# The head of a Mamba2-and-MLP kernel: C of the first chunk in one transfer and turned by TensorE, weight loads issued by ScalarE, mixing moved up

## The chip, the cores and the metric

The kernel runs on one core of a Trainium2 chip. The metric is the device time of one execution in microseconds (us). Engine names in the profile: PE is TensorE's matmuls, PEld its weight loads, DVE is VectorE, ACT ScalarE, POOL GpSimd, SP SyncE, which issues most DMAs. "L585" is line 585 of the kernel before, and matmuls of fp32 leave two records each, as do their weight loads.

## The reference

Two blocks follow one another. A state-space block works on 4 batches, 8 heads, 768 positions, head size 32, state size 16; then an MLP works on 3,072 tokens of 256 values.

```python
# per chunk of the sequence; cum = cumsum of log(a) in the chunk
L  = exp(cum[i] - cum[j]) for i >= j, else 0
y  = ((C @ B.T) * L) @ x  +  (C @ state) * exp(cum)
state = exp(sum(log a)) * state + sum_j exp(cum[-1] - cum[j]) * B[j] x[j]
# MLP
h = y.reshape(3072, 256) @ w_in          # 256 x 2048
g = h * clip(h + 3, 0, 6) / 6
out = g @ w_out                          # 2048 x 256
```

x, B, C and the result are float32; w_in and w_out arrive as 64-bit floats.

## The kernel before

The work goes through six chunks of 128 positions, each with all 4 batches and 8 heads. A chunk is two halves of 64. Its state-space part gives 512 columns of y, and the MLP part of that chunk follows: 16 blocks of 128 hidden values (`mlp_in` for chunk 0, `lead` and `follow` later), then the products with w_out. TensorE goes through the MLP of chunk k while the other engines prepare chunk k+1.

The order on each engine is written out by hand (`manual_schedule`): every engine takes its instructions in the order in which the program issues them. What the change touches is the head, ahead of chunk 0's MLP (L969 to L1018), where nothing can hide behind earlier matmuls:

- `load_bc(c)` loads B and C. B of chunk 0 goes over ScalarE's DMA queue. C of chunk 0 comes "pairs first", with eight DMAs of 32 KB on SP (L104); VectorE then turns it with one 32x32 block transpose (`turn_squares`, L481) into csT, from which `part_heads` makes the two halves of cT (L488). Chunks 1 and 2 load C "tokens first" in one DMA (L97) and let TensorE transpose it (`turn_c`, L449).
- `diff_mask`, `diff` and `diff_exp` make the decays L of chunks 0 and 1 on TensorE and ScalarE: a mask, one matmul that subtracts, and 16 small ones per batch that add (L352, L364, L373), then exp (L381). `first_eto` does the same for the decay from the chunk's middle. Chunk 1's batches 2, 3 are exponentiated in the head, 0 and 1 during chunk 0's MLP.
- `add_up` is a scan on VectorE, first for chunks 0 and 1, later for the rest; `store_rows` writes the rest to DRAM, and `turn_cum` and `by_token` (L329, L332) turn it for later chunks.
- `ends` scales B by the decay on GpSimd (L412), `fade` scales csT by eto (L494), `scores` makes C B^T and the states (L543, L555), `multiply` puts the decays on (L585), `mix` makes y (L611 with x, L516 with the state), `keep` copies y to yT (L625), `renew` makes the new state.
- `load_w(i)` loads a megabyte of weights into one of three buffers: i = 0 to 3 the quarters of w_in, 4 to 7 those of w_out. `decode(i)` turns the 64-bit floats into fp32 in steps that `weights(i, n)` issues n at a time: a copy of the top 16 bits on ScalarE (L206), two masks on VectorE (L223, L225) and two instructions for the factor (L209, L213), two activations on ScalarE (L229, L231), then L236 and L249 on VectorE. Loads 4 and up are issued when the buffer's earlier user is decoded (L234).
- `busy` is a filler matmul of 128x512 into a free bank.
- PSUM tiles with the tags f0 to f3 share four banks; a new tile of a tag waits until the old one is read.

## Time and profile before

| | us |
|---|---|
| median of 3 runs | 345.6 (345.52 to 349.03) |
| the profiled execution | 345.45 |
| its span, first to last instruction | 343.7 |
| PE busy / share | 334.6 / 97% |
| VectorE busy / share | 220.1 / 64% |
| ScalarE busy / share | 173.2 / 50% |
| GpSimd busy / share | 142.7 / 42% |
| first L636 (chunk 0's MLP) starts | 22.98 |
| first L735 (chunk 0 times w_out) starts | 50.55 |

How to read it: times inside the profile count from the span's start. The chain of waits is followed back from the last instruction; its lines give start, length and what ran. A timeline line gives start, length, engine, line, operation, tiles, and in brackets how long the engine sat idle before it and what ended that. Busy shares are means over stages with different limits.

### The profile page before, as it was taken

What the parts mean: (1) busy time and instruction counts of PE and PEld (TensorE: products, weight loads), DVE (VectorE), ACT (ScalarE), POOL (GpSimd) and SP (SyncE); (2) the same over time, 40 slices, a digit from 0 to 9 for tenths busy, and PEclk for the clock granted to TensorE, in tenths of its full rate; (3) what the DMA queues carried; (4) which work ended last, traced back from release to release, by engine and by line L of the source; (5) the groups of instructions that cost most, each with busy time, mean ns of one, the idle gap of its engine ahead of it and who ended that gap; (6) DMA issues with size and microseconds to landing.
All of it is one profiled execution on the core that took longest, in us unless ns stands there. A gap on an engine that the chain in (4) does not pass through costs nothing.

```text
span 343.7 us, 8181 instructions
## 1 busy us (share of the span) xinstructions
PE 334.6 (97%) x3378; PEld 266.5 (78%) x3378; DVE 220.1 (64%) x357; ACT 173.2 (50%) x359; POOL 142.7 (42%) x139
## 2 busy tenths in 40 slices
PE   6889999999999999999999999999999999999996
PEld 2554448888778888888888888888887788888995
DVE  6689999999698647775438666447666324676011
ACT  4769878738874561564551564561564010565000
POOL 3300000093299923099611199610099400089500
PEclk9999999999999999999999999999999999999999
DMA  8888959206941057242029242051200010200010
GB/s 173 163 341 169 242 187 176 53 2 95 192 61 23 5 69 159 34 60 51 2 34 176 46 56 58 6 64 17 34 13 0 2 19 1 34 12 2 0 33 31
DMA packets 91605, 24.89 MB, mean 72 GB/s; under 512 B 84208, under 2 KB 87952, under 8 KB 91056
## 3 DMA queue, kind: packets, MB, share of 16 engines
q1 hardware_dynamic: 87184, 23.06, 34.8%
q10 hardware_dynamic: 4384, 1.31, 1.7%
q8 instruction: 26, 0.43, 0.5%
q14 instruction: 11, 0.09, 0.1%
HBM read 21.07 MB, written 3.29 MB: 71 GB/s over the span
## 4 chain that ended last, share of the span: by engine, by line
PE 75%; issue 11%; DMA 4%; DVE 2%; ACT 2%; POOL 2%; SPq 2%; POOLq 0%; DVEq 0%
PE h L684 31%; PE wb L861 13%; PE wc L861 8%; PE wa L861 8%; PE oa L794 4%; PE ob L794 4%; PE y L611 2%; PE y L516 2%; DMA raw<-in_moe_w_in_dram 2%; PE cb L543 2%; DMA eto<-cum_e 1%; ACT L L401 1%; POOL bs L412 1%; DMA pairs<-in_C_dram 1%; SPq L321 1%
## 5 line engine op out<-in xcount | busy, mean ns | idle before, releaser
L708 DVE SCALAR_TENSOR_TENSOR gT<-gT,h 128x512 f32<-128x512 f32 x80 | 54.9, 687 | 30.7 <-ACT gT L707 27.9
L707 ACT ACTIVATE gT<-h,half_up 128x512 f32<-128x512 f32 x80 | 55.1, 690 | 33.2 <-PE h L684 33.1
L780 POOL TENSOR_TENSOR s<-gT 128x512 f32<-128x512 f32 x20 | 25.8, 1288 | 66.4 <-DVE gT L708 66.4
L684 PE MATMUL h<-gap,w_gap 128*128 128x512 f32 x160 | 51.8, 409 | 0.0
L684 PE MATMUL h<-high,w_high 128*128 128x512 f32 x160 | 50.7, 398 | 0.1
L684 PE MATMUL h<-low,w_low 128*128 128x512 f32 x160 | 50.3, 395 | 0.0
L700 ACT ACTIVATE h<-h 128x512 f32<-128x512 f32 x40 | 23.5, 588 | 30.4 <-PE h L684 30.4
L684 PEld LDWEIGHTS h<-high,w_high 128*128 128x128 f32 x160 | 29.5, 188 | 8.5 <-DVE h L697 2.1
L684 PEld LDWEIGHTS h<-low,w_low 128*128 128x128 f32 x160 | 30.1, 188 | 7.2
L684 PEld LDWEIGHTS h<-gap,w_gap 128*128 128x128 f32 x160 | 29.9, 188 | 7.1 <-DVE gap L678 0.5
L401 ACT ACTIVATE L<-L,cum_n 128x64 f32<-128x64 f32 x128 | 31.6, 337 | 0.7 <-POOL L L162 0.7
L861 PE MATMUL wb<-s,w_out 128*128 128x256 f32 x128 | 30.7, 382 | 0.0
L419 POOL TENSOR_TENSOR tmp<-state,eto 128x256 f32<-128x256 f32 x5 | 3.6, 721 | 61.0 <-ACT eto L405 60.9
L735 PE MATMUL o<-w_out,gT 128*128 128x256 f32 x128 | 28.7, 381 | 0.0
L697 DVE TENSOR_SCALAR h<-h 128x512 f32<-128x512 f32 x40 | 27.7, 692 | 1.2 <-PE h L684 1.2
L636 PE MATMUL h<-yT,w 128*128 128x512 f32 x64 | 27.7, 594 | 0.0
L780 POOL TENSOR_TENSOR s<-s,gT 128x512 f32<-128x512 f32 x20 | 26.9, 1345 | 1.6
L585 DVE TENSOR_TENSOR L<-L,cb 128x512 f32<-128x512 f32 x24 | 15.3, 682 | 19.1 <-PE cb L543 16.3
L735 PEld LDWEIGHTS o<-w_out,gT 128*128 128x128 f32 x128 | 24.1, 190 | 3.8 <-issue 0.5
L861 PEld LDWEIGHTS wb<-s,w_out 128*128 128x128 f32 x128 | 24.0, 190 | 3.6
L412 POOL TENSOR_TENSOR bs<-B,L 128x128 f32<-128x128 f32 x24 | 13.7, 584 | 30.9 <-ACT L L401 25.8
L780 POOL TENSOR_TENSOR gT<-gT 128x512 f32<-128x512 f32 x20 | 25.9, 1294 | 0.0
(141 smaller groups left out, 534.3 us busy)
## 6 DMA issues: line engine op xcount, KB each, us to landing
raw<-in_moe_w_out_dram SPq DMA_DIRECT2D x4, 1024.0 KB
L<-cum_d SPq DMA_DIRECT2D x8, 512.0 KB
xt<-in_x_dram SPq DMA_DIRECT2D x6, 512.0 KB
raw<-in_moe_w_in_dram SPq DMA_DIRECT2D x3, 1024.0 KB
out_dram<-back SPq DMA_DIRECT2D x128, 16.0 KB
eto<-cum_e SPq DMA_DIRECT2D x20, 64.0 KB
B<-in_B_dram SPq DMA_DIRECT2D x5, 256.0 KB
raw<-in_moe_w_in_dram ACTq DMA_DIRECT2D x1, 1024.0 KB
```

The source lines that it names most:

```text
L401: nc.scalar.activation(Ls[c][:, b, h], Ls[c][:, b, h], AF.Exp, bias=cum_n[:, c, g:g + 1])
L412: nc.gpsimd.tensor_tensor(out=bss[c][:, hs], in0=Bs[c][:, hs], in1=Ls[c][:, b, :, HT - 1:HT].to_broadcast([P, NH, N]), op=ALU.mult)
L636: nc.tensor.matmul(out=h.rearrange("p r i -> p (r i)"), lhsT=first_in[f // FP][:, j, f % FP * P:(f % FP + 1) * P], rhs=yTs[k][:, j], start ...
L684: nc.tensor.matmul(out=h, lhsT=w[:, j, f * P:(f + 1) * P], rhs=y[:, j], start=(start and j == 0), stop=True, skip_group_check=True)
L697: nc.vector.tensor_scalar(out=h, in0=h, scalar1=-Z / UP, scalar2=None, op0=ALU.mult)
L700: nc.scalar.mul(h, h, -Z / UP)
L707: nc.scalar.activation(g, h, AF.Relu, bias=half_up, scale=UP * UP / 6.0)
L708: nc.vector.scalar_tensor_tensor(out=g, in0=g, scalar=UP, in1=h, op0=ALU.min, op1=ALU.mult)
L735: nc.tensor.matmul(out=o[:, b % 2], lhsT=gTs[0][:, f, b * P:(b + 1) * P], rhs=w_out[:, f], start=(f == 0 and b % 2 == 0), stop=True, skip_ ...
L780: nc.gpsimd.tensor_tensor(out=o, in0=p_, in1=q_, op=op)
L794: nc.tensor.matmul(out=bank[:, slot], lhsT=lhs[:, j], rhs=rhs[:, j], start=(clear and j == 0), stop=True, skip_group_check=True)
L861: nc.tensor.matmul(out=bank[:, slot], lhsT=lhs[:, j], rhs=rhs[:, j], start=(clear and j == 0), stop=True, skip_group_check=True)
```

## The change

C of chunk 0 is loaded tokens first in one DMA, as chunks 1 and 2 have it, and TensorE turns it, together with B and the later chunks' sums, behind the first half (batches 2, 3) of chunk 1's differences. The second half of those differences (batches 0, 1) moves from before the scores to before the mixing. GpSimd makes the second half of csT out of cT's two halves. The loads 1, 2, 3 are issued by ScalarE, not SP, and at other places. The factor's two instructions of decode 1 are issued with its first step, and this whole first step goes behind `keep`. `by_token` goes from VectorE to ScalarE. Mixing and copying alternate by halves. The fillers go.

```diff
-        if 0 < c < TURN:
+        if c < TURN:
             bcs[c] = [tokens_first(C, name="C", tag="bc")]
         Bs[c] = tokens_first(B, nc.scalar if c == 0 else nc.sync, name="B")
-        if c == 0:
-            bcs[c] = [pairs_first(C), Bs[c]]
-        elif c < TURN:
+        if c < TURN:
             bcs[c].append(Bs[c])
...
     load_w(0, nc.scalar)
     load_bc(0)
     load_x(0)
-    load_w(1)
...
         parts_m = significand()
-        if i == 0:
+        if i < 2:
             next(parts_m)
             next(parts_m)
...
     def by_token(c_ps):
-        nc.vector.tensor_scalar(
-            out=cum_n[:, 2:], in0=c_ps[:, 2:], scalar1=-1.0, scalar2=None, op0=ALU.mult)
+        nc.scalar.mul(cum_n[:, 2:], c_ps[:, 2:], -1.0)
...
+    def fade_end(c):
+        _, cT, csT = (t[..., HALF[1]] for t in turned(c))
+        nc.gpsimd.tensor_tensor(out=csT, in0=cT[:, :, 0], in1=cT[:, :, 1], op=ALU.add)
+        nc.gpsimd.tensor_tensor(out=csT, in0=csT, in1=etos[c][:, :, HALF[1]], op=ALU.mult)
...
-    def keep(c):
-        yTs[c] = y_tile("yT", FP32)
-        for u in range(2):
-            for a in range(2):
-                nc.scalar.copy(out=y_half(yTs[c], a, u), in_=ys[c][a, u])
+    def keep(c, u):
+        for a in range(2):
+            nc.scalar.copy(out=y_half(yTs[c], a, u), in_=ys[c][a, u])
...
     first_eto()
     diff(1, 2, 3)
+    diff_exp(1, 2)
+    diff_exp(1, 3)
     weights(0, 1)
+    add_up(ends_at[1])
+    store_rows()
+    turn_c(0, turn_ps(0, 0))
+    turn_b(0)
+    c_ps = ps.tile([P, NC, G], FP32, name="c_ps", tag="f3")
+    turn_cum(c_ps)
+    by_token(c_ps)
     for b in range(NB):
         ends(0, b)
-    turn_b(0)
-    diff(1, 0, 1)
-    busy(1, ps.tile([P, NB * P], FP32, name="d", tag="f0"))
+    load_w(1, nc.scalar)
     weights(0, 1)
-    diff_exp(1, 2)
-    diff_exp(1, 3)
-    turn_squares(bcs[0][0], turned(0)[2])
-    part_heads(0)
-    fade(0, HALF[1], nc.gpsimd)
-    add_up(ends_at[1])
-    store_rows()
-    load_w(2)
+    fade_end(0)
     weights(0, 1)
     scores(0)
     multiply(0)
-    load_w(3)
-    c_ps = ps.tile([P, NC, G], FP32, name="c_ps", tag="f1")
-    turn_cum(c_ps)
-    busy(1, ps.tile([P, NB * P], FP32, name="d", tag="f0"))
+    load_w(2, nc.scalar)
     weights(0, 1)
+    diff(1, 0, 1)
+    yTs[0] = y_tile("yT", FP32)
+    mix(0, (0,))
+    keep(0, 0)
+    mix(0, (1,))
+    keep(0, 1)
     weights(1, 1)
-    by_token(c_ps)
-    mix(0)
-    keep(0)
+    load_w(3, nc.scalar)
     weights(1, 3)
     renew(0)
     weights(1, 1)
```

More of the change, by code (lines that the diff above doesn't have):

```diff
@@ L432, in turn_ps @@
         if c < 2:
-            return ps.tile([P, NB, P], FP32, name="t_ps", tag=f"f{2 * j if c else 1}")
+            return ps.tile([P, NB, P], FP32, name="t_ps", tag=f"f{2 * j if c else 1 + j}")
         return ps_o.tile([P, NB, P], FP32, name="t_ps", tag="o")
@@ L490, in part_heads, with fade @@
                 op0=ALU.mult)
-    def fade(c, sl=slice(0, P), engine=nc.vector):
-        csT = turned(c)[2][:, :, sl]
-        engine.tensor_tensor(out=csT, in0=csT, in1=etos[c][:, :, sl], op=ALU.mult)
+    def fade(c):
+        csT = turned(c)[2]
+        nc.vector.tensor_tensor(out=csT, in0=csT, in1=etos[c], op=ALU.mult)
+    def fade_end(c):
+        _, cT, csT = (t[..., HALF[1]] for t in turned(c))
+        nc.gpsimd.tensor_tensor(out=csT, in0=cT[:, :, 0], in1=cT[:, :, 1], op=ALU.add)
+        nc.gpsimd.tensor_tensor(out=csT, in0=csT, in1=etos[c][:, :, HALF[1]], op=ALU.mult)
     def turn_all(c):
@@ L501, in turn_all @@
         fade(c)
-    def busy(n, bank):
-        for _ in range(n):
-            nc.tensor.matmul(
-                out=bank.rearrange("p (b i) -> p b i", b=NB), lhsT=ident,
-                rhs=ident.unsqueeze(1).to_broadcast([P, NB, P]), start=True, stop=True)
     def from_state(c, a, pairs=range(NQ)):
```

## The prediction

> **What bounds the kernel now.** I read the page first, then the chain of waits in order of time, then the timelines of TensorE, VectorE and ScalarE up to 84 us, and the trace's records of DMA packets. The page says that PE is busy for 334.6 of 343.7 us; a list of all of PE's waits has five entries, all before 21 us. So what the head of the kernel gains reaches the end only if nothing behind it makes PE wait anew. The chain through the head:

> ```profile
> 8.67 3.78 DMA pairs<-in_C_dram
> ...
> 12.63 1.18 DVE csT L481
> 13.81 0.02 issue
> 13.83 0.89 DVE cT L488 x2
> 14.73 0.14 issue
> 14.86 1.25 PE cb L543 x61
> 16.11 0.01 issue
> 16.12 1.30 DVE L L585 x2
> 17.41 0.04 issue
> 17.46 0.43 PE c_ps L329 x4
> 17.88 1.05 PE d L506 x2
> 18.94 0.87 PE y L611 x52
> 19.80 0.93 issue
> 20.74 0.30 PE y L611 x4
> ```

> C lands last, VectorE turns it, then come scores, decay product, a filler matmul, the mixing. In the mixing PE stops for 0.93 us though nothing it needs is missing ("issue"). From there it is 2.33 us to the last state matmul (20.74 to 23.07), and the wide matmuls L636 run from 23.

> The second bound does not show in PE's waits. VectorE, from its timeline:

> ```profile
> 25.73 0.69 DVE L236 TENSOR_TENSOR wse<-wse 128x1024 uint16<-128x1024 uint16 x1 [1.43 <-ACT wse L231]
> 26.46 1.23 DVE L249 SCALAR_TENSOR_TENSOR w<-wm,wse 128x1024 f32<-128x1024 f32 x1
> ...
> 48.57 1.22 DVE L249 SCALAR_TENSOR_TENSOR w_out<-wm,wse 128x1024 f32<-128x1024 f32 x1
> ```

> From 25.73 to 73.2 VectorE has one gap of 0.62 us. At 49.80 it finishes the first quarter of w_out, and PE takes that up at 50.55:

> ```profile
> 22.98 27.73 PE L636 MATMUL h<-yT,w 128*128 128x512 f32 x64
> 50.55 15.70 PE L735 MATMUL o<-w_out,gT 128*128 128x256 f32 x72
> ```

> So PE has only 0.75 us of slack over VectorE at 50.55 us. (The fourth quarter of w_in, ready at 42.79 and wanted at about 43.8, has 1.0.)

> **The 0.93 us stop.** The page lists this queue:

> ```profile
> q8 instruction: 26, 0.43, 0.5%
> ```

> PE has 6,756 records; 26 packets is one for about 260 of them, so q8 feeds PE's program. The stop comes at PE's 705th record. The second packet starts at 18.50 us and takes 0.95; PE goes on at 20.74, 2.24 us after the start. The other packets mostly start about 1.1 us after PE is 64 records short of a page's border; this one starts 3.1 us after it, just as the 4,096-byte packets of w_in's second part (14.8 to 18.6 us) end. The third likewise starts at 24.09, as those of the third and fourth part end. I read: a large load ahead of it holds the program's packet back.

> **The change, part by part.**

> *C in one transfer.* Eight DMAs whose issues fill SP from 1.27 to 9.22 become one issue (0.46 us, as for chunk 1's C); x is issued right behind it, not at 9.27. C is then 4,096 pieces of 64 bytes beside as many of B. B's parts on twelve engines land by 8.71 us, and on the four that also carry C's pieces by 10.82. Ends for C: 8.71, and 12.3 (B's first packet at 5.1 and twice its 3.6 us). I take up to 11.2, near B's crowded engines; until then PE is in chunk 1's differences (to 11.22) anyway. x landed at 15.44 and should by 13.

> *Turning by TensorE.* Out: the VectorE transpose (1.17). In: four transposes, 0.44 us from 11.16; B's follow to 12.04, the four of c_ps to 12.48. The scan is now ahead of cT on VectorE, from 10.3 to 11.5, while it used to wait for C; c_ps and the stores of cum_e and cum_d get it 4 us sooner. cT is read from PSUM: two instructions between 0.48 (L488, from SBUF) and 0.69 (L697, from PSUM) each, the latter taken: 11.9 to 13.2, instead of 14.71. ScalarE: two exponentials to 12.2, bT 0.59, cum_n between 0.32 (L580) and 0.37 (L571), done near 13.2. Scores from 13.35, not 14.86: **1.5 us earlier**. The products follow to 17.1, not 18.60.

> *GpSimd* now adds the two halves of cT before fading: one more instruction, between 0.62 (L419) and 1.50 (L494), so done between 14.6 and 16.3. Needed by the state matmuls, after 17.3: nothing. The copies of B by decay (4 times 0.41) wait for B and are done by 12.5, for a need at 14.5.

> *Chunk 1's second differences* (34 matmuls, 1.22 us) move from before the scores to before the mixing: 15.2 to 16.45, while VectorE multiplies until 17.1, so half covered. The two fillers (1.12 each) go. **Mixing starts at 16.45, not 18.87.** ScalarE's copies for it are done by 16.4 (decode's two, 1.15 each, from 13.0; then 0.37 and two of 0.32).

> *Loads on ScalarE.* The second part is issued behind cum_n, at 12.55 (0.44, as w0's issue; ScalarE's next work has slack), 1.1 us before the end of its issue on SP (14.12). The third goes behind the copies near 16, the fourth behind decode 1's first copy, where ScalarE waits 0.5 us for VectorE anyway; if it blocks, 0.45 us follow in the decode. SP loses three issues; its w_out load waits for that copy, near 23.4, as before.

> *Where the program's packet lies.* Matmuls up to the stop, before: 8+2+34+34+4+34+4+34+2+64+64+4+2+60 = 350. After: 8+2+34+34+4+34+4+4+4+64+64+34+60 = 350. The stop stays at the end of the first mixing half, reached at 17.33 instead of 19.81. Before, the packet started 4.4 us after the load's issue ended (14.12 to 18.50). After: 13.0+4.4 = 17.4, and PE goes on at 17.4+2.24 = 19.64. Its ends: 15.5 (asked for and served at once: no stop), and 20.1 (held by the third part too, 2.7 us more: two loads take 5.4 back to back). I take 17.4, the nearest row. Last state matmul: 19.64+2.33 = 21.97, **1.10 us earlier**.

> [...]

> *Decode of the second part.* Its first copy (1.13) now stands behind the four yT copies, and VectorE's mask (0.42) waits for it. Before: L236 at 25.73, 2.66 after the last state matmul. After: +0.29 yT, +1.13 copy, +0.06 and 0.42 mask, +0.05, then 1.15, 0.04, 1.15, 0.03: 4.32 after it. The factor's two instructions (0.69, 1.23), put ahead, are on VectorE from 19.0 to 20.9 and hide behind PE's stop. So VectorE's full stretch starts 4.32-2.66 = **1.66 us later relative to PE**: 21.97+4.32 = 26.29 instead of 25.73, 0.56 late.

> **Sum.** VectorE's w_out quarter comes at 49.80+0.56 = 50.36; the 0.75 of slack is used up: gain = 1.10-1.66+0.75 = 0.2 us. The profiled execution took 345.45 (span 343.7 and 1.75 around it), 0.15 under the median of the three runs. Forecast 345.45-0.2 = **345.2 us**.

> **Rivals.**
> 1. *The forecast*: the page stop stays and PE waits again at w_out. Its own range: packet from 16.8 to 18.1, gain 0.8 to -0.5: 344.7 to 345.9. Chance 0.52.
> 2. *The packet comes in time.* For: most of the 26 do. Against: both that met a large load were late. Last state matmul 17.33+2.33 = 19.66, 3.41 earlier; through VectorE 3.41-1.66+0.75 = 2.5 is left: 343.0. Chance 0.20.
> 3. *Slower: the packet waits for the third part too*, as this is now queued at 16, right behind the second. For: the third packet of before outwaited two loads. Start 20.1, last state matmul 24.7, 1.6 later; VectorE 3.3 late, less 0.75: 2.5 us slower, 348.0. It decides from a start later than 17.6, where the gain is zero. Chance 0.13.
> 4. *The clock falls.* Without fillers PE idles for 2.3 us. Its first masks took 0.43 each, two later ones of that shape 0.60 together, though the page's granted clock is full. If it fell for 3.4 to 5.4 us (2.14 to at most 7.56 at the start), L636 loses 1.7 to 2.7: 346.1 to 347.1. The longest stop before is 0.93, so no row settles it. Chance 0.06. [...]
> 5. *The change doesn't do what it says*: C in 4,096 small pieces lands at 12.4 as now. All is 1.3 us later than in 1: 346.5. Chance 0.06.
> Rest 0.03.

> **Numbers.** 345.2 is case 1. The range, 342.7 to 347.3, takes in cases 1, 2, 4, 5 and leaves out most of 3 and the rest. Faster or slower means by over 1% (3.45 us, about what a measurement can tell from no change): no case gets there. Faster would need 3.41 us with no VectorE bound, 0.03; slower needs case 3 and another, or a ScalarE queue blocked by its loads (SP was once, 4.08 us), 0.07; within 1%, 0.90.

> **What would show it.** Right: C's transposes at 11.2, scores near 13.4, mixing near 16.5; PE then stops about 2.3 us with no releaser, until 19.6; L236's successor near 26.3; a new PE wait on VectorE at about 49.5 to 50.4. Wrong: no stop near 17.3 (case 2); a stop past 20 (case 3); L636 matmuls at double length (case 4); PE waiting for C past 11.5 (case 5); or PE waiting elsewhere between 66 and 84 us, where GpSimd's instructions stretch from 0.41 to 1.39 beside VectorE's.

## The result, and the profile after

The changed kernel takes 346.56 us (median of 21 runs, 346.24 to 348.88) against 345.52 (21 runs, 344.68 to 349.03): 1.0 us more, ratio 1.0038 with a 95% interval of 1.002 to 1.0057. The forecast was 345.2, 0.3 below the kernel before. The time lies in the given range and is "within 1%", but it moved to the other side. One run is in no ratio of this document, the sixth of e10_load_later: it took 428.61 us at a mean granted clock of 0.747, where all others had at least 0.98.

The profiled execution took 347.64 (span 345.9, before 343.7). In it TensorE's clock was halved for 10.24 us in the head (mean granted clock 0.985). The five of the 21 runs with a clock of 1.000 took 346.38 to 346.55, so the median does not come from the clock. I read the profile beside a second one of the same kernel (run `e0_again`: 346.64 us, span 344.9, clock 0.994). The first one's page, with PE's busy time and the row of the clock (tenths of full speed in 40 slices of the span; the 5 lies in the halved stretch):

```profile
span 345.9 us, 8175 instructions
...
PE 336.5 (97%) x3378; PEld 268.5 (78%) x3378; DVE 219.3 (63%) x355; ACT 173.2 (50%) x360; POOL 142.2 (41%) x140
...
PEclk9959999999999999999999999999999999999999
```

PE's timeline in the second profile:

```profile
11.35 0.63 PE L434 MATMUL t_ps<-ident,C 128*128 128x128 f32 x4 [0.26 <-DMA C<-in_C_dram]
...
13.57 1.20 PE L538 MATMUL cb<-cT,bT 32*64 32x128 f32 x64 [0.80 <-DVE cT L453]
14.90 0.44 PE L550 MATMUL y<-xt,bs 64*32 64x64 f32 x29
16.53 0.85 PE L550 MATMUL y<-xt,bs 64*32 64x64 f32 x35 [1.19 <-issue]
17.31 1.03 PE L360 MATMUL d<-less,split 128*128 128x512 bf16 x2
18.28 1.06 PE L369 MATMUL d<-split,pick 128*64 128x64 bf16 x32
19.27 1.30 PE L606 MATMUL y<-L,xt 64*32 64x64 f32 x64
...
22.51 1.98 PE L629 MATMUL h<-yT,w 128*128 128x512 f32 x4
```

C is turned at 11.35 and the scores start at 13.57, nearly as forecast. Then PE stops for 1.19 us with nothing missing ("issue"), but inside L550 (its 449th record), not in the mixing (its 705th). Mixing starts at 19.27, later than before (18.87), and has no stop in it. The wide matmuls start at 22.51, 0.47 us earlier than before. Up to 0.2 of this can be the clock's own start: it is first full at 6.22 us here and at 7.09 in the profile before, and the kernel before starts them at 22.77 where the clock is full at 6.24 (e7_or_twice, whose edit acts later).

ScalarE and then VectorE in the second profile, around the second part's decode:

```profile
22.62 0.37 ACT L618 COPY yT<-y 128x256 f32<-128x256 f32 x1 [0.26 <-PE y L511]
...
22.89 1.12 ACT L203 COPY wse<-raw 128x1024 uint16<-128x1024 uint16 x1
24.51 1.15 ACT L226 ACTIVATE wse<-wse,bias_hi 128x1024 bf16<-128x1024 uint16 x1 [0.49 <-DVE wse L220]
25.69 1.15 ACT L228 ACTIVATE wse<-wse,bias_lo 128x1024 uint16<-128x1024 bf16 x1
```

```profile
24.04 0.43 DVE L220 TENSOR_SCALAR wse<-wse 128x1024 uint16<-128x1024 uint16 x1 [3.00 <-ACT wse L203]
...
26.87 0.69 DVE L233 TENSOR_TENSOR wse<-wse 128x1024 uint16<-128x1024 uint16 x1 [0.95 <-ACT wse L228]
```

The copy L203 stands behind the last yT copy, and VectorE idles 3.00 us for it. L233 (L236 before) starts at 26.87 instead of 25.73: 1.14 us late. In the first profile it starts at 27.90, 2.17 late. The spans are 1.2 and 2.2 us longer. What VectorE is late by, the whole kernel is late by. About 1.0 of the 2.17 comes ahead of the decode, from the halved clock: the last state matmul ends at 23.62 there, at 22.58 in the second profile.

### The profile page after: what moved, and what is told of

It reads as the page before. It is cut to its first block, busy times and chain, and to the rows that moved or that the text cites. A ratio compares the mean times of both kernels' runs of the same rounds, so it can differ in the third digit from the quotient of the medians.

```text
span 345.9 us, 8175 instructions
## 1 busy us (share of the span) xinstructions
PE 336.5 (97%) x3378; PEld 268.5 (78%) x3378; DVE 219.3 (63%) x355; ACT 173.2 (50%) x360; POOL 142.2 (41%) x140
## 4 chain that ended last, share of the span: by engine, by line
PE 76%; issue 11%; ACT 3%; DMA 3%; DVE 3%; POOL 2%; SPq 1%; POOLq 0%; ACTq 0%
PE h L677 31%; PE wb L854 12%; PE wc L854 8%; PE wa L854 8%; PE oa L787 4%; PE ob L787 4%; PE y L606 2%; DMA eto<-cum_e 2%; PE y L511 2%; PE cb L538 2%; ACT L L397 1%; POOL bs L408 1%; PE y L550 1%; DMA pre<-in_a_dram 1%; POOL L L159 1%
## 5 line engine op out<-in xcount | busy, mean ns | idle before, releaser
L629 PE MATMUL h<-yT,w 128*128 128x512 f32 x64 | 29.1, 616 | 0.0
L728 PE MATMUL o<-w_out,gT 128*128 128x256 f32 x128 | 28.7, 381 | 0.0
L580 DVE TENSOR_TENSOR L<-L,cb 128x512 f32<-128x512 f32 x24 | 15.3, 682 | 20.0 <-PE cb L538 17.2
L728 PEld LDWEIGHTS o<-w_out,gT 128*128 128x128 f32 x128 | 24.1, 190 | 3.8 <-issue 0.5
L408 POOL TENSOR_TENSOR bs<-B,L 128x128 f32<-128x128 f32 x24 | 13.7, 584 | 32.1 <-ACT L L397 26.1
```

Of the source, the lines that this page charges most:

```text
L408: nc.gpsimd.tensor_tensor(out=bss[c][:, hs], in0=Bs[c][:, hs], in1=Ls[c][:, b, :, HT - 1:HT].to_broadcast([P, NH, N]), op=ALU.mult)
L629: nc.tensor.matmul(out=h.rearrange("p r i -> p (r i)"), lhsT=first_in[f // FP][:, j, f % FP * P:(f % FP + 1) * P], rhs=yTs[k][:, j], start ...
L728: nc.tensor.matmul(out=o[:, b % 2], lhsT=gTs[0][:, f, b * P:(b + 1) * P], rhs=w_out[:, f], start=(f == 0 and b % 2 == 0), stop=True, skip_ ...
```

## Where the slack was not

The forecast took VectorE's last border to be the first w_out quarter, with 0.75 us of slack. Following the chain of waits of the kernel before past 66 us shows another:

```profile
68.99 4.48 POOL bs L412 x4
73.47 1.10 POOL L L162
...
78.47 1.29 ACT L L401 x5
...
82.73 0.70 DVE gap L678
83.43 0.04 issue
83.48 0.97 PE h L684 x3
```

GpSimd's four `bs` take 1.39, 0.41, 1.39 and 1.39 us here (0.41 each in the head, where VectorE stands idle beside them). The long ones run beside VectorE's `w_gap` and `w_low`, and the fourth ends at 73.47, 0.27 us after the last L663 on VectorE:

```profile
71.77 1.43 DVE L663 SCALAR_TENSOR_TENSOR w_gap<-w_high,w 128x1024 fp32r<-128x1024 f32 x1
```

In both profiles of the changed kernel and in those of e1, e5, e7, e9 and e11 it ends 0.26 to 0.28 us after the same instruction, early or late, so VectorE's lateness passes on to GpSimd in full. From there a chain goes through the mask, chunk 2's exponentials, `high`, `low` and `gap` to PE. `gap` ends at 83.42. PE's matmul ahead of it starts at 82.85 and ends at 83.43 (0.58, its length in the fence below). Slack: nothing. No list of waits shows it, because PE waits 0.05 us. In the second profile of the changed kernel the same chain is late by 1.14, and the wait is there:

```profile
43.97 7.13 PE L629 MATMUL h<-yT,w 128*128 128x512 f32 x16 [0.36 <-DVE w L246]
51.07 5.20 PE L728 MATMUL o<-w_out,gT 128*128 128x256 f32 x23
...
83.45 0.58 PE L677 MATMUL h<-gap,w_gap 128*128 128x512 f32 x1
84.62 0.96 PE L677 MATMUL h<-gap,w_gap 128*128 128x512 f32 x3 [0.59 <-DVE gap L671]
```

These lines are PE's timeline. The fourth w_in quarter makes it wait 0.36, the first w_out quarter (51.07) nothing visible, `gap` 0.59. That was an inference from two profiles; the runs below test it. Three explanations competed: the order of the decode with no slack behind it, the clock, and PE's stop at record 449 in the head. The letters of the theories hold only inside the expectation that they stand in.

## Experiments

The runs stood on three chips, e0 to e3 on one, e5 to e8 on a second, e9 to e12 on a third. Each ratio here is against the kernel before on the same chip (345.54, 35 runs; 345.56, 25 runs; 345.37, 25 runs).

**e0_again**: the changed kernel once more.

> The changed kernel unchanged, for a second profile and more times. Theory A (clock): the granted clock falls to half for some 10 us around the mixing, and that is the loss; then executions at clock 1.000 should take no longer than the kernel before, 345.5. Theory B (decode order): the first copy of decode 1 behind the yT copies makes VectorE late, and PE waits for w_out at about 50 us; then executions at clock 1.000 take about 346.4 too, and a profile at full clock shows PE waiting for VectorE at the first L728. Theory C (program's packets): the stop of 1.2 us at the 449th PE record costs about 1 us in every execution; the profile shows a stop without releaser in L550, near 15.3 us, again.

Measured: 346.72 us (346.48 to 348.67, 12 runs; before on this chip 345.54, 35 runs; ratio 1.0032, 0.9997 to 1.0067). Its profile was read above. Runs at a clock of 1.000 took 346.48 to 346.66: about 1.1 us over the kernel before without any clock fall. PE waited for VectorE, but at the fourth w_in quarter and at `gap`, not at the first L728.

**e1_copy_first**: the changed kernel with the second part's first decode step ahead of the mixing.

```diff
     weights(0, 1)
+    weights(1, 1)
     diff(1, 0, 1)
...
     keep(0, 1)
-    weights(1, 1)
     load_w(3, nc.scalar)
```

> The changed kernel with one part undone: decode 1's first copy (and with it the factor's two instructions) is issued ahead of the mixing again, so that ScalarE does it before the yT copies. Theory B: the decode's last step comes 2.66 us behind the last state matmul and not 4.3, 1.6 us sooner, and the time falls by 0.8 to 1.6 us, to 345 or less. Theory A: no change, 346.5, since PE still loses its clock and is the bound. Theory C: no change, 346.5, the stop at the 449th record stays at 1.2 us.

Measured: 345.2 us (12 runs, 344.79 to 349.27; ratio to before 1.0, 0.9959 to 1.0042), 1.5 us under the changed kernel on the same chip. The runs at a clock of 0.999 or more took 344.79 to 345.31, those of the changed kernel 346.48 to 346.66. Its profile (345.0, span 343.3, clock 1.000), VectorE and then PE:

```profile
25.24 0.69 DVE L233 TENSOR_TENSOR wse<-wse 128x1024 uint16<-128x1024 uint16 x1 [2.28 <-ACT wse L228]
```

```profile
16.50 0.57 PE L550 MATMUL y<-xt,bs 64*32 64x64 f32 x35 [1.23 <-issue]
...
18.16 0.81 PE L606 MATMUL y<-L,xt 64*32 64x64 f32 x58
20.08 0.31 PE L606 MATMUL y<-L,xt 64*32 64x64 f32 x6 [1.11 <-issue]
```

L233 comes 0.49 earlier than before, the span is 0.4 shorter. The order of that one copy is the loss. What is left of the head's gain is cut by two stops put down to "issue", 1.23 us at record 449 and 1.11 at record 705, where the kernel before has one of 0.93.

**e2_filler**: the changed kernel with a 128x256 filler matmul ahead of the scores.

```diff
     by_token(c_ps)
+    busy(1, ps.tile([P, 2 * P], FP32, name="d", tag="f0"), 2)
```

> The changed kernel with one filler matmul of 128x256 (0.56 us) in PE's gap ahead of the scores. Theory A: executions with a mean clock under 1.000 become rare, those of 347.3 to 348.9 go away, the profile shows clock 1.000 and the median falls by 1 us or more, to about 345.5. Theory B: the long executions go away, but the median stays near 346.4. Theory C: as B; the page's border comes four records earlier in the program, and the stop stays.

Measured: 346.71 us (12 runs, 346.15 to 348.96; ratio 1.0018, 0.9984 to 1.0052): no better, and the profiled run (348.64, clock 0.984) had the clock halved twice. The clock is under 0.999 in 5 of the 12 runs (7 of 12 in e0_again), too few to tell the two apart, but the seven others take 346.15 to 347.02, so the loss stays without a fall. The filler takes 0.70 us, and PE still waits 0.17 for cT. In this profile PE has no stop at record 449 and one of 1.66 us in the mixing.

**e3_x_rows**: the changed kernel with x of the first chunk read as 128 contiguous rows of 4 KB instead of pieces of 128 bytes. It computes with other values of x there.

```diff
+        if c == 0:
+            nc.sync.dma_start(
+                out=xts[c].rearrange("s g d -> s (g d)"),
+                in_=x[0].rearrange("h s d -> (h s d)")[:P * NB * NH * D].rearrange("(s f) -> s f", s=P))
+            return
```

> The changed kernel with chunk 0's x loaded as 128 rows of 4,096 bytes (the first 512 KB of x as they lie, which are other values than chunk 0's, so y and the output differ) and not as 4,096 pieces of 128 bytes: the same bytes, a sixteenth or less of the packets. Theory C: the first packet of PE's program starts near 10.7 us, as before the change, and not at 13.6; the stop at the 449th record goes, and the last state matmul comes 1 us or more sooner; the time falls by up to that, to 345.4, as far as decode 1 lets it. Theory A: with less idling the clock holds; the same time as C for a clock of 1.000. Theory B: the head gains, but the bound is VectorE, whose decode follows the last state matmul by 4.3 us; PE waits at the first L728 and part of the gain is lost.

Measured: 347.64 us (12 runs, 345.83 to 348.74; ratio 1.0032, 0.9995 to 1.0069), all with a clock under 0.999. PE's timeline:

```profile
15.65 0.60 PE L366 MATMUL d<-less,split 128*128 128x512 bf16 x2
...
16.81 0.81 PE L612 MATMUL y<-L,xt 64*32 64x64 f32 x58
19.83 0.31 PE L612 MATMUL y<-L,xt 64*32 64x64 f32 x6 [2.21 <-issue]
```

This is the head that I forecast: mixing at 16.81 (forecast 16.45), PE on at 19.83 (19.64). The first program packet starts at 12.02 us, against 13.65 in the changed kernel and 10.64 before, and the stop at record 449 is gone. In the trace's packet records it starts as x's transfer ends: in the changed kernel when 4,077 of x's 4,096 pieces have started, here 0.05 us after the last row of x (11.97). The profile of e5 shows the same on the kernel before: there x's first pieces were ahead (10.66), and the packet starts at 13.96, behind 3,922 of them (in e9, with 116 ahead, at 11.04). I read: x, now issued at 1.73 instead of 9.27 us, holds the packet that PE needs for record 449. With its small pieces the packet starts at 13.65 and PE stops for 1.2 us; with rows it starts at 12.02 and PE does not stop there.

The four runs left two questions: is the order of the copy enough by itself, and is there really no slack? e5, e7 and e9 ask them on the kernel before.

**e5_copy_late**: the kernel before, with only the first decode step of the second part moved behind `keep`.

```diff
-    weights(1, 1)
     by_token(c_ps)
     mix(0)
     keep(0)
+    weights(1, 1)
```

> The kernel before, with one part of the change alone: the first step of the second part's decode (ScalarE's copy of 1.13 us) stands behind the yT copies. Its head is as before. Theory A (VectorE has no slack at the end of its stretch, near 83 us): L233 starts about 4.3 us after the last state matmul instead of 2.66, the second gap comes 1.0 to 1.7 later, and the time is 1.0 to 1.6 us above the kernel before: 346.5 to 347.1. Theory B (0.75 us of slack at the first w_out quarter, as forecast): 0.3 to 0.9 above: 345.8 to 346.4. Theory C (the loss is in the head, not in this order): no change, 345.3 to 345.7.

Measured: 347.83 us (8 runs, 347.49 to 348.78; before 345.56, 25 runs; ratio 1.006, 1.0039 to 1.0082). That is 2.3 up, more than any theory said. The factor's two instructions (0.69 and 1.23) had lain in VectorE's idle time and now stand between the masks and L236, which starts at 29.04, 3.31 late; the profiled span is 3.3 longer. Of the 3.31, 0.87 is not the edit's: in this profile the clock is first full at 11.12 us (7.09 before), PE's stop in the mixing takes 1.29 us instead of 0.93, and the wide matmuls start at 23.85 instead of 22.98. The other 2.44 fit the median. The edit was not what I meant, as the changed kernel issues the factor earlier, so I repeated it (e9).

**e7_or_twice**: the kernel before, with L236 of the second part done twice (the expectation also calls it L233, its line in the changed kernel).

```diff
-        nc.vector.tensor_tensor(out=e, in0=e, in1=s, op=ALU.bitwise_or)
+        for _ in range(2 if i == 1 else 1):
+            nc.vector.tensor_tensor(out=e, in0=e, in1=s, op=ALU.bitwise_or)
```

> The kernel before, with VectorE's L233 of the second part done twice (the same OR again, 0.69 us more ahead of L236, output unchanged). It delays VectorE's stretch by 0.69 us and touches nothing else. Theory A (no slack at 83 us): first w_out and second gap both 0.6 to 0.7 later, the time 0.6 to 0.7 up: 346.1 to 346.3. Theory B (slack of 0.75): no change of the time, 345.3 to 345.7, and PE's wait at the first w_out quarter still absent.

Measured: 346.16 us (12 runs, 345.65 to 349.2; ratio 1.0017, 0.9993 to 1.0042, so the median alone does not decide). The eight runs at a clock of 0.999 or more have a median of 345.99, the 18 such runs of the kernel before 345.44: 0.55 up. The profiled span is 344.3, 0.6 longer. The profile shows where, VectorE and then PE:

```profile
25.52 1.42 DVE L237 TENSOR_TENSOR wse<-wse 128x1024 uint16<-128x1024 uint16 x2 [1.38 <-ACT wse L231]
```

```profile
82.83 0.58 PE L685 MATMUL h<-gap,w_gap 128*128 128x512 f32 x1
83.97 0.97 PE L685 MATMUL h<-gap,w_gap 128*128 128x512 f32 x3 [0.56 <-DVE gap L679]
```

PE takes up w_out at 50.46 without a wait, as the 0.75 of slack would have it. But the 0.52 us by which VectorE is later (the second OR ends at 26.94, the only one before at 26.42; the OR adds 0.73, and the decode starts 0.21 earlier in this profile) become 0.56 us of new waiting for `gap`.

**e6_no_filler**: the kernel before without its two filler matmuls.

```diff
-    busy(1, ps.tile([P, NB * P], FP32, name="d", tag="f0"))
...
-    busy(1, ps.tile([P, NB * P], FP32, name="d", tag="f0"))
```

> [...] Theory A (the removal of the fillers is not what costs): within 0.3 us of the kernel before, 345.2 to 345.8, and the granted clock falls in about as many of its runs (a third). Theory D (the removed fillers let the clock fall): half clock near 16 to 26 us in the profile, falls in most runs, the median 1 to 3 us up: 346.5 to 348.5.

Measured: 349.9 us (6 runs, 349.56 to 350.48; ratio 1.012, 1.0094 to 1.0146), 4.3 up, with a clock of 0.98 to 0.99 in all six; of the 25 runs of the kernel before beside them, 7 were under 0.999. So the fillers of the kernel before do help to hold the clock, and losing them costs more than expected. The profile's windows, cut where the granted clock steps (columns: length, busy PE, PEld, DVE, ACT, POOL, then the clock, the DMA share and GB/s):

```profile
13.12:16.54 3.42, 1.82 (x128) 1.68 (x128) 3.10 (x5) 2.13 (x4) 1.50 (x1) 1.00 0.96 165
16.54:19.95 3.41, 1.38 (x85) 1.02 (x68) 3.38 (x6) 1.79 (x4) 0.00 (x0) 1.00 1.05 391
19.95:23.36 3.41, 2.39 (x84) 2.14 (x86) 3.34 (x7) 1.01 (x4) 0.00 (x0) 0.50 1.02 416
```

**e8_rows_copy_first**: the edits of e1 and e3 together (other values of x in the first chunk).

> The changed kernel with two edits at once: the second part's first decode copy ahead of the mixing (as in the kernel before), and x of the first chunk read as 128 contiguous rows, so that the small pieces that held the program's first packet are gone (its x is other values). With the small pieces gone there was no stop at record 449 and mixing came at 16.81. Theory A (the order of the copy and the held packet are the two losses, and VectorE has no slack to hide either): last state matmul near 22, L233 near 24.8 to 25.1, the time 0.4 to 1.0 us below the kernel before: 344.5 to 345.1, in runs with a full clock. Theory C (the head's time is lost elsewhere, the stop at record 705 takes what the one at 449 gave): no better than with the copy moved alone, 345.1 to 345.5.

Measured: 346.84 us (12 runs, 344.45 to 348.16; ratio 1.0022, 0.9996 to 1.0047). Three runs kept the clock at 1.000 and took 344.45, 344.46 and 344.65, some 0.9 under the kernel before at that clock (median near 345.5). In the other nine it fell, for 6.83 us in the profiled one. By these three runs the head's gain reaches the end once both losses are gone, but the clock fell in three runs of four; in the profiled one it fell after a stretch of 3.41 us in which PE was busy for 1.14.

**e9_copy_late_factor**: e5 as it was meant, with the factor ahead as in the changed kernel.

```diff
-        if i == 0:
+        if i < 2:
...
-    weights(1, 1)
     by_token(c_ps)
     mix(0)
     keep(0)
+    weights(1, 1)
```

> The kernel before with the decode order of the changed one, both halves of it: ScalarE's first copy of the second part behind the yT copies, and the two instructions of the factor ahead of the masks, which the earlier run with the copy alone left behind them (there L236 came 5.2 us after the last state matmul, at 29.04). Theory A: L236 comes about 4.3 us after the last state matmul, 1.0 to 1.7 us later than in the kernel before, and the time follows one for one: 1.0 to 1.7 up, 346.5 to 347.2. Theory B (slack of 0.75 at the first w_out quarter): 0.3 to 0.9 up, 345.8 to 346.4. Both say that it is better than the copy alone (347.8).

Measured: 347.02 us (12 runs, 346.46 to 347.5; before 345.37, 25 runs; ratio 1.0025, 0.9998 to 1.0053), 1.65 up, one of the twelve with a clock under 0.999. The interval just touches one, but all twelve lie above the 18 lowest of the 25 runs before. ScalarE, VectorE and PE:

```profile
23.25 1.12 ACT L206 COPY wse<-raw 128x1024 uint16<-128x1024 uint16 x1
```

```profile
27.23 0.69 DVE L236 TENSOR_TENSOR wse<-wse 128x1024 uint16<-128x1024 uint16 x1 [0.95 <-ACT wse L231]
```

```profile
84.95 0.96 PE L684 MATMUL h<-gap,w_gap 128*128 128x512 f32 x3 [0.56 <-DVE gap L678]
```

L236 is 1.50 late, the span 1.5 longer. This part of the change alone costs more than the whole change does.

**e10_load_later**: e1 with the second w_in load issued beside the third one.

```diff
-    load_w(1, nc.scalar)
     weights(0, 1)
     fade_end(0)
...
     multiply(0)
+    load_w(1, nc.scalar)
     load_w(2, nc.scalar)
```

> The changed kernel with the copy ahead of the mixing, and in it the second w_in load issued about 3.5 us later, beside the third one, so that no large transfer runs when PE asks for the program's second packet. Theory E (the load of 1 MB holds that packet): the packet's start moves from 17.65 to about 16.5 to 17, and the stop at record 705 (1.11 us) is gone or under 0.5; since the second part then lands some 3 us later, VectorE's L233 comes 1 to 3 us later and the time is 1 to 3 us up: 346 to 348. Theory F (the packet is asked for only when PE passes record 449, at 16.5): it starts at 17.6 as before and the stop stays at about 1.1 us.

Measured: 349.16 us (6 runs; five of 347.79 to 350.08 at a clock of 0.989 to 0.995; ratio 1.0098, 1.0069 to 1.0127). The second part lands so late that ScalarE waits 4.47 us for it ahead of all four yT copies, and PE 1.5 us for these. The 4,096-byte packets now start at 18.39 us; the program's second packet starts at 17.89, with no large load beside it, and the stop at record 705 is still there:

```profile
16.74 0.57 PE L550 MATMUL y<-xt,bs 64*32 64x64 f32 x35 [1.13 <-issue]
...
20.59 0.31 PE L606 MATMUL y<-L,xt 64*32 64x64 f32 x6 [1.39 <-issue]
```

In these lines PE passes record 449 at 16.74, and the packet starts 1.15 us later; in e1 it is 16.50 and 17.65, in the changed kernel 16.49 and 17.63. So where PE has stopped at record 449, the next packet starts 1.14 to 1.15 us after PE has gone on, in e10 without a load that could hold it. Where PE did not stop there, the packet mostly starts as the load's last packet does (18.50 and 18.32 before, 17.60 and 17.58 in e3, but 19.20 and 17.88 in e5). That the load holds it in this case stays an inference, as no run without a stop at record 449 moved the load.

**e12_relu_first**: e1 with the masks and the first ReLU of the second part also ahead of the yT copies. **e11_relu_filler**: the same with e2's filler.

```diff
     mix(0, (0,))
+    weights(1, 2)
     keep(0, 0)
...
-    weights(1, 3)
+    weights(1, 1)
```

> The changed kernel with the copy ahead of the mixing, and with the second part's masks and its first ReLU (ScalarE, 1.15 us) also ahead of the yT copies, in ScalarE's idle time between 20.05 and 21.8. VectorE's L233 then comes at 24.1 to 24.3 instead of 25.24; the yT copies are at most 0.2 us later for PE. Theory A (two chains meet near 83 us; with the copy moved PE waits only 0.2 there, so PE's own work bounds): 0.1 to 0.4 us under the kernel with the copy moved alone, 344.8 to 345.1 in runs at a full clock. Theory G (VectorE's chain alone sets the end): a full 1.0 us less, 344.0 to 344.3.

> As the run with the first ReLU moved ahead, and a filler matmul of 128x256 in the 0.80 us in which PE waits for cT ahead of the scores. Theory D (the missing fillers let the clock fall): fewer of its runs have a granted clock under 0.999 than of the same kernel without it, median 344.8 to 345.2. Theory H (the page stops of 1.1 to 1.2 us let it fall, which no filler reaches): as many as without it, and the time the same or up to 0.4 us more.

Measured: e12 348.97 us (6 runs, clock 0.989 or 0.99 in all; ratio 1.0082, 1.005 to 1.0114), e11 347.98 (12 runs, 345.76 to 349.11; 1.0059, 1.0032 to 1.0085). Neither shows what was asked. ScalarE in e11:

```profile
21.71 1.15 ACT L226 ACTIVATE wse<-wse,bias_hi 128x1024 bf16<-128x1024 uint16 x1 [1.68 <-DVE wse L220]
...
22.77 1.18 ACT L625 COPY yT<-y 128x256 f32<-128x256 f32 x4
```

The ReLU waits 1.68 us for the masks, which stand behind the factor on VectorE; I had counted them ahead of it. All four yT copies come after the ReLU, and the wide matmuls wait for them (23.45 instead of 22.33 in e1). L233 comes at 25.02, 0.71 earlier than before, and the span (344.2) is 0.5 longer all the same, as are the wide matmuls' starts (23.45, 22.98). Here PE's own chain is the later one. The clock fell in 6 of 6 and in 9 of 12 runs (under 0.999), so one filler does not hold it here either; whether the missing fillers or PE's stops (two of 1.1 us in e11's profile) let it fall was not settled.

VectorE's lateness against the span, profiles with a clock of at least 0.999, and the two of the changed kernel:

| run | L236/L233 against before (us) | span against before | median of the runs at a clock of 0.999 or more, against before's |
|---|---|---|---|
| e1_copy_first | -0.49 | -0.4 | -0.39 |
| e7_or_twice (end of the second OR) | +0.52 | +0.6 | +0.55 |
| e0_again (clock 0.994) | +1.14 | +1.2 | +1.13 |
| e9_copy_late_factor | +1.50 | +1.5 | +1.68 |
| changed kernel (clock 0.985) | +2.17 | +2.2 | not known |
| e5_copy_late (0.87 of it a later head) | +3.31 | +3.3 | +2.35 |
| e11_relu_filler (PE's chain) | -0.71 | +0.5 | +0.67 |

The last column takes 3 runs in e11 and 5 to 11 in the others, so the match does not rest on single profiles.

## Why the prediction was wrong, step by step

- *C in one transfer, turning by TensorE*: right. C's transposes at 11.35 to 11.48 (forecast 11.16), scores at 13.6 to 13.7 (13.35).
- *Mixing at 16.45*: wrong by 2.8 us (19.27, and 19.23). The step assumed x's early issue free. With it the program's first packet starts 3 us later (13.65, not 10.64), and PE stops 1.2 us at record 449, earlier than any stop that I considered. e1, with the same stop and a full clock, has mixing at 18.16, so 1.1 of the 2.8 is the halved clock: from the end of the stop to the mixing it is 2.74 us in e0_again, 1.66 in e1. e3 takes the stop away and has mixing at 16.81.
- *Where the program's packet lies* ("the stop stays at the end of the first mixing half"): wrong in place, nearly right in effect. The wide matmuls start 0.47 earlier in e0_again and 0.65 in e1, against the forecast 1.10. I had tied the packet to the load; e10 shows that after a stop at 449 the packet follows that stop. That it came at 17.63, near the forecast 17.4, was luck; in e3, without a stop at 449, the head came as this step has it.
- *Decode of the second part* (4.32 us behind the last state matmul instead of 2.66): right. 22.58 to 26.87 is 4.29.
- *Sum* ("the 0.75 of slack is used up"): **the step that turned the sign.** The slack exists at 50.55, but behind it `gap` at 83.4 has none. e7 and e9 show it on the kernel before. With zero slack the sum is 1.10-1.66 = -0.56; with the head's measured 0.47 it is -1.19, and e0_again's span is 1.2 longer. The step also passed over the fourth w_in quarter: by its own figures PE and VectorE move 1.10+0.56 = 1.66 towards each other, against a slack of 1.0 there, and e0_again waits 0.36 there and nothing visible at the w_out quarter.
- *Rival 2* (the packet comes in time, 343.0): half of it happened, as there is no stop at record 705; the stop at 449 had taken its place. *Rival 3* (held by the third load): did not occur. *Rival 5* (C no earlier, 346.5): no. The measured 346.56 beside its time, and inside that of rival 4, is luck.
- *Rival 4* (the clock falls, 346.1 to 347.1, chance 0.06): the chance was much too small. 16 of the 21 runs have a clock under 0.999, against 29 of the 85 runs of the kernel before that stood beside the experiments. Eight of the 16 take 347.29 to 348.88, the other eight 346.24 to 346.74, about as those at a full clock. So it raises eight of the 21 runs, and hardly the median. Its "longest stop before is 0.93" left out waits of 1.00 and 0.94 us for VectorE that the list of PE's waits holds. Its fall of 3.4 to 5.4 us was an estimate: the profile before has no fall, and no run shows one of 5.4. The others' heads show 3.41 (e0_again), 6.83 (e6_no_filler) and 10.24 (the changed kernel).
- The closing warning, "PE waiting elsewhere between 66 and 84 us, where GpSimd's instructions stretch", named the place. It should have been followed to its end, as its chain was in the profile before.

A kernel faster than both was not found. e8 points at one (about 0.9 us at a full clock), but x of the first chunk lies in pieces of 128 bytes, and an x load that spares the packet and keeps the clock was not tried.

## What to carry to other kernels

Before a delay is charged against slack, follow the delayed engine's whole chain to the last place where it meets the bounding engine: the smallest slack along it counts, and a meeting with a slack of zero shows in no list of waits. The chain of waits of the kernel before had it at 82.73 to 83.48. When one step goes behind another on a queue, the price is the whole dependent decode behind it, here 1.6 us for one copy of 1.12.

## What the runs showed of the hardware

In the head the clock is halved for 3.41 us (e0_again, e10_load_later), 6.83 (e3_x_rows, e6_no_filler, e8_rows_copy_first, e12_relu_first), 10.24 (the changed kernel), or 3.41 and later 6.83 (e2_filler): always multiples of 3.41, from another time in each execution. The clock is also first full at another time in each, 4.81 us (e2_filler) to 11.12 (e5_copy_late, where two matmuls L364 take 1.03 us at 9.30 and 0.59 at 11.36), and the head moved with it: the kernel before, with edits that do not touch PE's work up to there, starts its wide matmuls at 22.77 (full from 6.24, e7_or_twice), 22.98 (7.09) and 23.85 (11.12, e5_copy_late). The changed kernel's windows, cut at its steps of 3.41:

```profile
12.60:16.01 3.41, 1.87 (x97) 1.41 (x95) 2.00 (x4) 2.96 (x4) 2.12 (x4) 1.00 1.25 239
16.01:19.42 3.41, 2.93 (x85) 1.86 (x93) 3.38 (x6) 0.90 (x3) 0.00 (x0) 0.50 0.62 211
```

The program's packets: q8 has 26, of 16,384 bytes each, for PE's 6,756 records. That they are PE's program is an inference from this count, one for 260 records. Two of PE's stops lie 256 records apart (449 and 705 in e1; the prediction calls such a stretch a page). Behind a stop at record 449 the next packet starts 1.14 to 1.15 us after PE has gone on (the changed kernel, e1, e10). In the head a stop put down to "issue" cost between 0.89 us (e7_or_twice) and 2.27 us (e8_rows_copy_first) of PE's time.
